# Layer norm's ScalarE part moved behind the last quad's normaliser, and shared products moved behind a mask product, in a two-layer-pair attention kernel

## The chip, the cores and the metric

The kernel runs on one core of a Trainium2 chip. The metric is device time in microseconds (us) of one execution; runs are repeated and their median is compared. The engines are TensorE (PE, with its weight loads shown apart as PEld), VectorE (DVE), ScalarE (ACT), GpSimd (POOL) and SyncE (SP), which issues transfers.

## What is computed

The reference applies four blocks to 2048 tokens of width 640: A, B, A, B, each as x = x + block(layernorm(x)), both A with the same weights and both B too.

```python
x = x + _A_ref(_layernorm(x), A_mem0, A_Wq, A_Wk, A_Wv, A_Wo, seg)
x = x + _B_ref(_layernorm(x), B_wqkv, B_wo)
x = x + _A_ref(_layernorm(x), A_mem0, A_Wq, A_Wk, A_Wv, A_Wo, seg)
x = x + _B_ref(_layernorm(x), B_wqkv, B_wo)
```

Block A works on 64 segments of 32 tokens, one after the other. Eight memory rows stand ahead of each segment, so it has 40 rows; 32 heads of width 192 attend over these rows under a mask, and the first eight output rows become the memory of the next segment. That recurrence is what makes the segments sequential. Block B has 32 heads of width 20 and looks back over 8 positions at a distance of 2. The layer norm has no weights: (x - m) / sqrt(v + eps).

## The kernel before

**Lanes and steps.** Both layer pairs run at once, as two lanes of 40 columns: lane 0 is the first pair, lane 1 the second, three segments behind (LAG). A step `t` does block A of segment `t` in lane 0 and of segment `t - 3` in lane 1, and parts of block B of the two steps before. There are 67 steps with block A, 61 of them (t = 3 to 63) with both lanes, the others with one, and two more that only finish block B.

**Quads.** A step goes over 8 quads of 4 heads (i = 0 to 7). Of each quad it makes K, Q and V (`a_k`, `a_q`, `a_v`; tiles ps_k, ps_q, ps_v), the scores (`a_s`: ps_s), their exponential E on ACT (L269), and E times the mask, Em, on DVE (L272). Then come, one quad later, P times V (`a_pv`: ps_o), the normaliser R on ACT, and the normalised output OT on DVE (`a_norm`); and one quad later still the output projection (`a_o`), which adds all quads into one PSUM bank, ps_acc.

**Normaliser.** V's tile has columns of ones, so ps_o holds the softmax sums beside the outputs. ACT takes four logarithms of them into R (L289) and one Exp with a factor of -1 (L291), which gives the reciprocals. DVE multiplies: one main product over all 128 partitions (L299), and two shared products (L300, L301) for the chunk whose halves belong to two heads, on partitions 0 to 63 and 64 to 127. ps_o has one buffer of two PSUM banks; R, E and Em have one buffer each, OT has two.

**Layer norm.** `ln1` prepares the next step's input: sums of x and of its squares by matmuls with ones (ps_st, L338), then on DVE the mean and the variance (L345 to L348), on ACT a logarithm and an Exp (ln_v, ln_r, L349 and L351), which give 1/sqrt(v + eps), on DVE x minus the mean (ln_xc, L356), and in `ln1_apply` the product with ln_r into the next step's input hT (L362, two instructions).

**End of a step.** After quad 6 the function `step` goes on, written out by hand: K and Q of quad 7, P times V of quad 6, V of quad 7, normalisation of quad 6, scores of quad 7, projection of quad 5, `ln1`, P times V and normalisation of quad 7, projection of quad 6, `ln1_apply`, block B's V and K (ps_bv, ps_bk, copied by ACT to VTB and KB), projection of quad 7, the new memory into hT (L326), x + A (L374), block B's Q (ps_bq) and a transpose of its V (ps_bvt). The next step begins with K of quad 0.

**Order.** The loop stands under a manual schedule for all five engines: each engine runs its instructions in the order in which the Python code issues them, and waits by semaphores for the others.

**Weights.** Block A's weights are 64 half units of 480 KB. 32 of them stay in SBUF; the other 32 are loaded again in each step by SP (L191) into a ring of six buffers (w_ring). All PSUM tiles of projections, statistics and block B share four banks in turn.

Of the kernel before, what the change touches and what calls it, by code (L numbers as in the profile page):

```python
# [61 lines left out]
class Kernel:  # L62
# [228 lines left out]
        nc.scalar.activation(out=rf, in_=rf, func=ACT.Exp, scale=-1.0)  # L291
        self.ov, self.r = ov, r

    def a_norm(self, i):
        nc = self.nc
        ov, r = self.cols(self.ov), self.cols(self.r[:])
        ot = self.ap2.tile([P, 2, 3, NT], BF16, name="OT")
        oc = self.cols(ot[:])
        nc.vector.tensor_tensor(out=oc[:, :, 0:3:2], in0=ov[:, :, 0:4:3], in1=r, op=ALU.mult)  # L299
        nc.vector.tensor_tensor(out=oc[0:64, :, 1], in0=ov[0:64, :, 1], in1=r[0:64, :, 0], op=ALU.mult)  # L300
        nc.vector.tensor_tensor(out=oc[64:P, :, 1], in0=ov[64:P, :, 2], in1=r[64:P, :, 1], op=ALU.mult)  # L301
        self.ots[i] = ot

    def a_o(self, i):
        nc = self.nc
# [35 lines left out]
    def ln_small(self, ps):  # L341

        nc = self.nc
        m = self.ap2.tile([P, NX], F32, name="ln_m")
        nc.vector.tensor_scalar(out=m[:], in0=ps[:, 0:NX], scalar1=1.0 / D, scalar2=None, op0=ALU.mult)  # L345
        v = self.bp.tile([P, NX], F32, name="ln_v")
        nc.vector.tensor_tensor(out=v[:], in0=m[:], in1=m[:], op=ALU.mult)
        nc.vector.scalar_tensor_tensor(out=v[:], in0=ps[:, NX:2 * NX], scalar=1.0 / D, in1=v[:], op0=ALU.mult, op1=ALU.subtract)  # L348
        nc.scalar.activation(out=v[:], in_=v[:], func=ACT.Ln, bias=self.eps_t[:])  # L349
        r = self.ap2.tile([P, NX], F32, name="ln_r")  # L350
        nc.scalar.activation(out=r[:], in_=v[:], func=ACT.Exp, scale=-0.5)  # L351
        return m, r
# [23 lines left out]
        self.bsq = self.ln_sq(x1)  # L376

    def b_ln(self, b):
        self.bmr = self.ln_small(self.ln_stats(self.x1[b], self.bsq))

    def b_ln_apply(self, b):
        dst = self.h2T[:, :, 64 * (b % 2):64 * (b % 2) + NX].rearrange("p c (l n) -> p c l n", l=2)
# [129 lines left out]

    def ln1(self, t):
        x = self.xin[t % 2]
        self.amr = self.ln_small(self.ln_stats(x, self.asq))
        self.axc = self.ln_center(x, self.amr)

    def ln1_apply(self, t):
        self.ln_scale(self.axc, self.amr, self.lanes(self.hT[t % 2][:, 0:NC * NT])[:, :, :, NM:LT])
# [1 line left out]
    def prologue(self):  # L521
        nc = self.nc
        self.xt, self.x1, self.ots, self.qxs = {}, {}, {}, {}
        self.x_load(0)
        nc.sync.dma_start(out=self.m0T[:], in_=self.mem0)
        nc.vector.tensor_copy(out=self.lanes(self.hT[0][:, 0:NC * NT])[:, :, 0, 0:NM], in_=self.m0T[:])
        self.x_take(0)
        self.ln1_sq(0)
        self.ln1(0)
        self.ln1_apply(0)  # L530
        self.build_mask_a()

    def step(self, t):
        T = self.n_seg + LAG
        self.set_lanes(t)
        b1 = t - 1 if 0 <= t - 1 < T else None
        b2 = t - 2 if 0 <= t - 2 < T else None
        nt = t + 1
        a = t < T
        for i in range(NQUAD - 1):  # L540
            if a:
                self.a_k(i, t)
                self.a_q(i, t)
                self.a_v(i, t)
                if i == 6:
                    self.a_pv(5)
                if i >= 2:
                    self.a_o(i - 2)
                if 1 <= i < 6:
                    self.a_pv(i - 1)  # L550
            if i == 0 and b1 is not None:
                self.b_ln(b1)
            if b2 is not None and i == 4:
                self.b_pv()
            if a and i >= 1:
                self.a_norm(i - 1)
            if b2 is not None and i == 6:
                self.b_wo(b2)
            if b2 is not None:
                if i == 0:  # L560
                    self.b_qexp(0)
                if 1 <= i <= 3:
                    self.b_s(b2, 2 * i - 2)
                    self.b_s(b2, 2 * i - 1)
                    if i < 3:
                        self.b_qexp(i)
                if i == 5:
                    self.b_ot()
            if i == 3 and b1 is not None:
                self.b_ln_apply(b1)  # L570
            if a:
                self.a_s()
            if t == 1 and i in (0, 3):
                self.load_b_weights(i)
            if t == 1 and i == 4:
                self.build_masks_b()
            if i == 1:
                if nt % 4 == 0 and nt < self.n_seg:
                    self.x_load(nt // 4)
                yseg = t - 3 - LAG  # L580
                if yseg >= 0 and yseg % 4 == 3:
                    self.y_store(yseg // 4)
            if i == 5 and nt < self.n_seg:
                self.x_take(nt)
        if a:
            self.a_k(7, t)
            self.a_q(7, t)
        if nt < T:
            self.ln1_sq(nt)
        if a:  # L590
            self.a_pv(6)
            self.a_v(7, t)
            self.a_norm(6)
            self.a_s()
            self.a_o(5)
        if nt < T:
            self.ln1(nt)
        if a:
            self.a_pv(7)
            self.a_norm(7)  # L600
            self.a_o(6)
        if nt < T:
            self.ln1_apply(nt)
        if b1 is not None:
            self.b_v(b1)
            self.b_k(b1)
        if a:
            self.a_o(7)
            if nt < T:
                self.mem_out(t)  # L610
            self.b_x1(t)
        if b1 is not None:
            self.b_q(b1)
            self.b_vt()
# [73 lines left out]
```

## Time and profile before

| what | value |
|---|---|
| runs: median (lowest to highest) | 3399.81 us (3399.69 to 3404.87), 3 runs |
| profiled execution: time, span | 3403.72 us, 3402.0 us |
| busy share of the span | PE 97%, PEld 85%, DVE 59%, ACT 61%, POOL 2% |
| mean granted clock of TensorE | 0.990 |
| transfers | 1088.74 MB, 320 GB/s in the mean; the weight queue 89.7% of the 16 engines' time |
| a step with both lanes, from K of quad 0 to K of quad 0 | 49.89 us |

A timeline line reads: start in us, time in us, engine, line of the kernel, operation, written tile <- read tiles, shapes, and count of merged instructions; in square brackets the idle time of the engine ahead of it and what ended that. A waits line reads: who waited for whom, total us, times, the longest. Matmuls overlap and their ends are modelled: a matmul of 80 columns is shown with about 0.20 us and the next one starts 0.036 us after it, so idle time of PE is best taken from start to start.

### The profile page before, as it was taken

Reading aid. Unit: us, or ns where it says so; the run is one execution under the profiler, and the core shown is the slowest. Engines: PE = TensorE matmul, PEld = TensorE weight load, DVE = VectorE, ACT = ScalarE, POOL = GpSimd, SP = SyncE. Lnnn points to the kernel's source line nnn. Section 1 sums busy time; section 2 is a strip of 40 time slices with the busy share of each in tenths; the row PEclk is TensorE's granted clock in tenths of the full one; section 3 lists DMA queues with packets and bytes.
Section 4 is the critical chain, followed back from the end, with each engine's and each line's share of the span. In section 5 each row is a group of like instructions: output and inputs, shape, how many; then the busy total and the mean of one; then the engine's idle time right before and its main releaser. Section 6 shows DMA issues by size and latency. Waiting matters only on the chain.

```text
span 3402.0 us, 164520 instructions
## 1 busy us (share of the span) xinstructions
PE 3284.0 (97%) x72896; PEld 2881.7 (85%) x72896; DVE 2004.8 (59%) x5841; ACT 2059.0 (61%) x6366; POOL 62.9 (2%) x188
## 2 busy tenths in 40 slices
PE   6899999999999999999999999999999999999997
PEld 4788888888888888888888888888888888888876
DVE  2456665665665666566566566656656656665654
ACT  2556666666666666666666666666666666666654
POOL 2000000000000000000000000000000000000000
PEclk7999999999999999999999999999999999999998
DMA  9989999999999999999999999999999999999995
GB/s 391 371 311 318 328 315 317 328 319 315 319 324 316 318 328 317 315 328 317 314 321 323 318 318 325 311 317 328 315 319 318 321 315 317 330 315 316 325 352 189
DMA packets 316123, 1088.74 MB, mean 320 GB/s; under 512 B 35504, under 2 KB 35632, under 8 KB 315280
## 3 DMA queue, kind: packets, MB, share of 16 engines
q1 hardware_dynamic: 313632, 1069.86, 89.7%
q8 instruction: 569, 9.32, 1.1%
q0 software_dynamic: 1776, 8.36, 0.8%
q14 instruction: 146, 1.20, 0.1%
HBM read 1075.46 MB, written 2.62 MB: 317 GB/s over the span
## 4 chain that ended last, share of the span: by engine, by line
PE 88%; ACT 5%; DMA 2%; issue 2%; DVE 2%; SPq 0%; POOLq 0%; ACTq 0%; POOL 0%
PE ps_v L251 25%; PE ps_k L221 16%; PE ps_q L221 16%; PE ps_acc L312 15%; PE ps_o L285 4%; ACT R L289 2%; PE ps_s L266 2%; PE ps_s L267 2%; DMA w_ring<-in_A_Wv_dram 2%; PE ps_bq L392 2%; PE ps_bs L441 2%; PE ps_by L486 1%; PE ps_st L338 1%; DVE OT L299 1%; ACT R L291 1%
## 5 line engine op out<-in xcount | busy, mean ns | idle before, releaser
L299 DVE TENSOR_TENSOR OT<-ps_o,R 128x320 bf16<-128x320 f32 (+1 forms) x536 | 255.3, 476 | 960.9 <-ACT R L291 949.4
L289 ACT ACTIVATE R<-ps_o 64x160 f32<-64x160 f32 (+1 forms) x2144 | 625.5, 292 | 307.3 <-PE ps_o L285 247.2
L251 PEld LDWEIGHTS <-hT 128*128 128x128 bf16 x5360 | 494.6, 99 | 298.3 <-issue 16.5
L221 PEld LDWEIGHTS <-w_ring 128*128 128x128 bf16 x16080 | 633.5, 100 | 13.8 <-issue 7.5
L257 ACT CAST Vt<-ps_v 80x384 bf16<-80x384 f32 x536 | 253.0, 472 | 566.5 <-PE ps_v L251 566.5
L251 PE MATMUL ps_v<-w_ring,hT 128*128 128x384 bf16 x2680 | 530.0, 329 | 9.3 <-DMA w_ring<-in_A_Wv_dram 7.7
L251 PE MATMUL ps_v<-w_v,hT 128*128 128x384 bf16 x2680 | 528.8, 329 | 3.1 <-DMA w_v<-in_A_Wv_dram 3.1
L312 PE MATMUL ps_acc<-OT,w_ring 128*128 128x80 bf16 (+1 forms) x8040 | 459.5, 200 | 43.8 <-DVE OT L299 37.8
L312 PE MATMUL ps_acc<-OT,w_o 128*128 128x80 bf16 (+1 forms) x8040 | 457.7, 200 | 4.5 <-issue 3.2
L239 DVE CAST QT<-ps_q 128x480 bf16<-128x480 f32 (+1 forms) x536 | 340.3, 635 | 184.9 <-PE ps_q L221 174.6
L312 PEld LDWEIGHTS <-w_ring 128*128 128x128 bf16 x8040 | 371.4, 99 | 85.6 <-issue 50.1
L221 PE MATMUL ps_q<-hT,w_ring 128*128 128x80 bf16 (+1 forms) x8040 | 370.5, 200 | 7.6 <-DMA w_ring<-in_A_Wq_dram 4.1
L221 PE MATMUL ps_k<-hT,w_k 128*128 128x80 bf16 (+1 forms) x8040 | 370.7, 200 | 6.4 <-DMA w_k<-in_A_Wk_dram 4.0
L221 PE MATMUL ps_q<-hT,w_q 128*128 128x80 bf16 (+1 forms) x8040 | 370.1, 200 | 5.9 <-DMA w_q<-in_A_Wq_dram 5.1
L221 PE MATMUL ps_k<-hT,w_ring 128*128 128x80 bf16 (+1 forms) x8040 | 369.9, 200 | 4.1 <-DVE hT L362 2.1
L312 PEld LDWEIGHTS <-w_o 128*128 128x128 bf16 x8040 | 350.6, 100 | 6.3 <-issue 4.6
L255 DVE CAST Vt<-ps_v 80x384 bf16<-80x384 f32 x536 | 293.6, 548 | 58.7 <-PE ps_v L251 58.7
L221 PEld LDWEIGHTS <-w_k 128*128 128x128 bf16 x8040 | 316.3, 100 | 7.5 <-DMA w_k<-in_A_Wk_dram 4.6
L221 PEld LDWEIGHTS <-w_q 128*128 128x128 bf16 x8040 | 316.0, 100 | 6.8 <-DMA w_q<-in_A_Wq_dram 5.9
L232 ACT CAST KF<-ps_k 128x320 bf16<-128x320 f32 (+1 forms) x536 | 217.9, 407 | 110.8 <-PE ps_k L221 110.8
L291 ACT ACTIVATE R<-R 128x320 f32<-128x320 f32 (+1 forms) x536 | 245.4, 458 | 17.0
L285 PE MATMUL ps_o<-Em,Vt 80*128 80x80 bf16 (+1 forms) x4288 | 239.5, 199 | 2.2 <-DVE Em L272 0.3
(99 smaller groups left out, 4100.0 us busy)
## 6 DMA issues: line engine op xcount, KB each, us to landing
w_ring<-in_A_Wk_dram SPq DMA_DIRECT2D x536, 480.0 KB, 5.4
w_ring<-in_A_Wq_dram SPq DMA_DIRECT2D x536, 480.0 KB, 5.4
w_ring<-in_A_Wv_dram SPq DMA_DIRECT2D x536, 480.0 KB, 5.3
w_ring<-in_A_Wo_dram SPq DMA_DIRECT2D x536, 480.0 KB, 5.6
w_k<-in_A_Wk_dram SPq DMA_DIRECT2D x8, 480.0 KB, 9.6
w_q<-in_A_Wq_dram SPq DMA_DIRECT2D x8, 480.0 KB, 9.6
w_v<-in_A_Wv_dram SPq DMA_DIRECT2D x8, 480.0 KB, 9.8
w_o<-in_A_Wo_dram SPq DMA_DIRECT2D x8, 480.0 KB, 9.7
```

The costliest lines, as they stand in the source:

```text
L221: nc.tensor.matmul(ps[:, NT * n + self.c0:NT * n + self.c1], lhsT=w[:, c, P * (n % 3):P * (n % 3 + 1)], rhs=hT[:, NT * c + self.c0:NT * c ...
L232: nc.scalar.copy(out=kf, in_=pv[:, :, 0:3:2, :])
L239: self.nc.vector.tensor_copy(out=self.cols(qt[:]), in_=self.cols(ps[:, 0:6 * NT].rearrange("p (a n) -> p a n", a=6)))
L251: nc.tensor.matmul(ps[:, 0:384], lhsT=hT[:, NT * c:NT * c + P], rhs=w[:, c, :], start=(c == 0), stop=(c == NC - 1))
L255: nc.vector.tensor_copy(out=dst, in_=src)
L257: nc.scalar.copy(out=dst, in_=src)
L266: nc.tensor.matmul(self.cols(sv[:, h]), lhsT=kf[:, NT * h:NT * h + P], rhs=self.cols(qt[:, 3 * pr + 2 * j]), start=True, stop=False)
L285: nc.tensor.matmul(self.cols(ov[:, pr, k]), lhsT=vt[0:NT, 512 * pr + c0:512 * pr + c0 + P], rhs=self.cols(em[0:NT, 2 * pr + k // 2]), star ...
L289: nc.scalar.activation(out=self.cols(r[r0:r0 + 64, :, j]), in_=self.cols(src), func=ACT.Ln)
L291: nc.scalar.activation(out=rf, in_=rf, func=ACT.Exp, scale=-1.0)
L299: nc.vector.tensor_tensor(out=oc[:, :, 0:3:2], in0=ov[:, :, 0:4:3], in1=r, op=ALU.mult)
L312: nc.tensor.matmul(self.acc[:, NT * c + self.c0:NT * c + self.c1], lhsT=w[m // 3][:, m % 3, P * c:P * (c + 1)], rhs=self.cols(ot[:, m]), s ...
```

## The change

Three things are reordered. `ln_small` is split: the DVE part stays in `ln1`, and the ACT part (ln_v, ln_r) is a function of its own, `ln_rstd`, which `step` calls after P times V and the normaliser of quad 7. At the start of the program and in block B's layer norm the two parts still follow each other. `a_norm` is split: for quad 6 alone the main product comes first, then the scores of quad 7 with E and Em, then the two shared products. By the build, the order of instructions on PE, POOL and SP is the same as before; only ACT's and DVE's at the end of a step differ. No instruction is added or removed, and no transfer.

```diff
-    def a_norm(self, i):
+    def a_norm(self, i, split=False):
...
+        self.norm = ov, r, oc
         nc.vector.tensor_tensor(out=oc[:, :, 0:3:2], in0=ov[:, :, 0:4:3], in1=r, op=ALU.mult)
+        self.ots[i] = ot
+        if not split:
+            self.a_norm_mid()
+
+    def a_norm_mid(self):
+
+        nc = self.nc
+        ov, r, oc = self.norm
         nc.vector.tensor_tensor(out=oc[0:64, :, 1], in0=ov[0:64, :, 1], in1=r[0:64, :, 0], op=ALU.mult)
         nc.vector.tensor_tensor(out=oc[64:P, :, 1], in0=ov[64:P, :, 2], in1=r[64:P, :, 1], op=ALU.mult)
-        self.ots[i] = ot
...
         nc.vector.scalar_tensor_tensor(out=v[:], in0=ps[:, NX:2 * NX], scalar=1.0 / D, in1=v[:], op0=ALU.mult, op1=ALU.subtract)
+        return m, v
+
+    def ln_rstd(self, m, v):
+        nc = self.nc
         nc.scalar.activation(out=v[:], in_=v[:], func=ACT.Ln, bias=self.eps_t[:])
...
     def b_ln(self, b):
-        self.bmr = self.ln_small(self.ln_stats(self.x1[b], self.bsq))
+        self.bmr = self.ln_rstd(*self.ln_small(self.ln_stats(self.x1[b], self.bsq)))
...
     def ln1(self, t):
         x = self.xin[t % 2]
-        self.amr = self.ln_small(self.ln_stats(x, self.asq))
-        self.axc = self.ln_center(x, self.amr)
+        self.amv = self.ln_small(self.ln_stats(x, self.asq))
+        self.axc = self.ln_center(x, self.amv)
+
+    def ln1_rstd(self):
+        self.amr = self.ln_rstd(*self.amv)
...
         self.ln1(0)
+        self.ln1_rstd()
         self.ln1_apply(0)
...
         if a:
             self.a_pv(6)
             self.a_v(7, t)
-            self.a_norm(6)
+            self.a_norm(6, True)
             self.a_s()
+            self.a_norm_mid()
             self.a_o(5)
         if nt < T:
             self.ln1(nt)
         if a:
             self.a_pv(7)
+        if nt < T:
+            self.ln1_rstd()
+        if a:
             self.a_norm(7)
             self.a_o(6)
```

## The prediction

> **What bounds the kernel now.** I read the busy shares first, then the waits of TensorE (PE), then the end of one step in the timelines of PE, ScalarE (ACT) and VectorE (DVE). The engine bound is PE; this row is 50 us from the middle:
>
> ```profile
> core 0: us, PE busy (x) PEld busy (x) DVE busy (x) ACT busy (x) POOL busy (x), PEclk, DMA share, GB/s
> ...
> 1000.00:1050.00 50.00, 49.37 (x1096) 43.64 (x1093) 30.25 (x87) 31.33 (x96) 0.41 (x1) 1.00 0.92 318
> ```
>
> PE is idle for 0.63 of 50 us, at full clock. The waits between 300 and 3300 us name one cause:
>
> ```profile
> PE ps_acc L312 <- DVE OT L299: 34.4, 58, 0.6
> PE ps_acc L312 <- issue: 5.3, 9, 1.1
> ...
> PE ps_o L285 <- DVE Em L272: 0.3, 1, 0.3
> ```
>
> So once in a step of 49.89 us the output projection waits 0.6 us for a normalised tile, and no weight transfer is waited for. The PE timeline of one step's end has it at quad 7:
>
> ```profile
> 1028.22 0.31 PE L338 MATMUL ps_st<-xin,ones 128*128 128x64 bf16 x5
> 1028.37 0.31 PE L338 MATMUL ps_st<-sq,ones 128*128 128x64 bf16 x5
> 1028.70 0.46 PE L285 MATMUL ps_o<-Em,Vt 80*128 80x80 bf16 x8
> ...
> 1030.81 1.04 PE L392 MATMUL ps_bk<-h2T,wqkv_sb 128*128 128x64 bf16 x30
> 1032.44 0.52 PE L312 MATMUL ps_acc<-OT,w_ring 128*128 128x80 bf16 x10 [0.60 <-DVE OT L299]
> ...
> 1033.51 1.04 PE L392 MATMUL ps_bq<-h2T,wqkv_sb 128*128 128x64 bf16 x30
> 1034.39 0.44 PE L420 MATMUL ps_bvt<-ident,VTB 128*128 128x128 bf16 x5
> ```
>
> The ends of matmuls are modelled, so I count from start to start. Thirty matmuls of this shape take 0.88 us (ps_bq to ps_bvt), so ps_bk leaves PE free at 1030.81 + 0.88 = 1031.69; the projection starts at 1032.44, a wait of **0.75 us**. A second one hides before ps_o: ten ps_st matmuls at 0.029 us leave PE free at 1028.51, and ps_o starts at 1028.70, 0.19 us later. No other change of group in the step has such a hole. Why quad 7 is late, ACT and DVE tell:
>
> ```profile
> 1027.47 0.43 ACT L269 ACTIVATE E<-ps_s 80x320 bf16<-80x320 f32 x1
> 1029.49 0.35 ACT L349 ACTIVATE ln_v<-ln_v,eps_t 128x64 f32<-128x64 f32 x1 [1.58 <-DVE ln_v L348]
> 1029.87 0.26 ACT L351 ACTIVATE ln_r<-ln_v 128x64 f32<-128x64 f32 x1
> 1030.14 1.23 ACT L289 ACTIVATE R<-ps_o 64x160 f32<-64x160 f32 x4
> 1031.40 0.47 ACT L291 ACTIVATE R<-R 128x320 f32<-128x320 f32 x1
> ```
>
> ```profile
> 1027.24 0.49 DVE L299 TENSOR_TENSOR OT<-ps_o,R 128x320 bf16<-128x320 f32 x1 [0.44 <-ACT R L291]
> 1027.65 0.30 DVE L300 TENSOR_TENSOR OT<-ps_o,R 64x160 bf16<-64x160 f32 x1
> 1027.97 0.33 DVE L301 TENSOR_TENSOR OT<-ps_o,R 64x160 bf16<-64x160 f32 x1
> 1028.33 0.32 DVE L272 TENSOR_TENSOR Em<-E,maskA 80x320 bf16<-80x320 bf16 x1
> ...
> 1031.90 0.49 DVE L299 TENSOR_TENSOR OT<-ps_o,R 128x320 bf16<-128x320 f32 x1 [2.04 <-ACT R L291]
> ```
>
> ACT sits idle 1.58 us for layer norm's variance, does ln_v and ln_r, and only then takes the logarithms of quad 7 (R, L289), though their ps_o was started at 1028.70.
>
> **Part 1: ln_v and ln_r behind R of quad 7.** Nothing is added or removed; the instruction orders of PE, POOL and SP stay, so no DMA is moved. Where ACT is free, R starts 0.54 us after ps_o (quad 6: 1024.94 to 1025.48). Here it starts 1.44 us after; 0.90 us goes from the chain. New chain, counted from ps_o: 0.54, four logarithms 1.26 (1030.14 to 1031.40), Exp to the main product 0.50 (to 1031.90), main product to the projection 0.54 (to 1032.44): **2.84 us**. PE itself is ready 1031.69 - 1028.70 = **2.99 us** after ps_o. So the chain falls 0.15 us behind PE's own work, and all of the 0.75 goes. What is late next is PE.
>
> What waits behind the moved pair: ln_r is wanted by DVE's hT products (L362), which stand behind the three products of quad 7 anyway: 1.80 + 0.50 + 0.41 + 0.32 + 0.36 = 3.39 us after ps_o, while ln_r is done by 1.80 + 0.50 + 0.38 + 0.26 = 2.94. Cover 0.45 us. Then VTB and KB on ACT: VTB now starts 3.07 us after ps_o and will start by about 3.0; the transposes that read it come 0.88 us after the projection's 1.07, near 4.9. Cover over 1 us. The next step's first matmuls need hT's memory columns (L326), which follow the projection and move with it; they end at 1033.95 against 1034.67. All three cost nothing; were the first cover gone, hT would start later by what is missing, with 0.7 us more before PE felt it.
>
> **Part 2: shared products of quad 6 behind Em of quad 7.** Em can start earlier, but ps_o lies in a single buffer, and the shared products (L300, L301) read quad 6's values from it. So ps_o of quad 7 has to wait for them as well, not for Em alone: a new wait, and PE is behind it. E ends at 1027.90, and Em starts 0.03 us after E where it waits for that alone (one-lane step: E ends at 3318.95, Em starts at 3318.98): 1027.93 to 1028.25, while the main product frees DVE at 1027.65. DVE idles 0.28 us there. Then the first shared product. It has no such predecessor in the trace, so there are two ends: it starts 0.08 us before Em's end, as it starts before the main product's (1027.65 against 1027.73, in all 488 two-lane cases), or 0.03 after, as the QT cast (L239) does behind Em in 304 cases. I take the first, since that row is the same instruction with the same operands, and the casts follow a shared product's read of rows 64 to 127. Then 1028.17; the second at +0.32, 1028.49; its end at +0.33, 1028.82; ps_o 0.06 later, as behind Em now: **1028.88 against 1028.70, 0.18 us later**. By the other end it is 1028.99, 0.29 later. It cannot fall below zero: Em and both products must end before ps_o, and the group gains an idle stretch.
>
> The Trainium skill, VectorE: DVE Perf Modes, section "Two Vector instructions with no wait between them", states a model by which an instruction waits for the one ahead to finish only when the start quadrant of an input or output differs from the last one used in that memory. The trace agrees where it can be seen (L301 starts 0.01 us after the end of L300, L300 starts 0.08 before the end of L299). By it the first shared product isn't held behind Em and the QT cast is, so it gives the 0.18; the nearest row after Em itself would give 0.29, 6.7 us more over the run.
>
> In the one-lane steps (t = 0 to 2 and 64 to 66), Em isn't what ps_o waits for: at t = 65 ps_o starts at 3319.32 with PE just free, and by the same count it would start near 3319.68; there the later projection waits only 0.05. Steps 1, 64 and 65 lose 0.3 to 0.4 each; steps 0 and 2, whose projections wait 1.7 and 0.8, gain 0.7 and 0.4; sum near 0, within 1 us.
>
> **The sum.** A two-lane step: 0.75 - 0.18 = 0.57, or 0.58 from unrounded times; there are 61 (t = 3 to 63): 35.4 us. Profiled execution: 3403.72 - 35.4 = 3368.3. That execution is 3.9 us above the median of the runs, and its step lengths show up to 1 us extra in some ten steps with no wait to name, so I set the forecast from the median: 3399.81 - 35.4 = **3364.4**. With the other end (0.29) it is 61 x 0.47 = 28.7, 3371.1.
>
> **Rivals.**
> *The stream of weights takes the gain.* Each step streams 32 x 480 KB = 15.7 MB, 315 GB/s over 49.89 us and 319 over 49.31. Against it: the first two 50 us windows moved 381 and 406 GB/s, PE waits for no transfer after 300 us, and each ring load there lands before its first matmul, 2 to 3 us in the median, 0.28 at the least. For it: the DMA share is 0.92, and a shorter tail gives less time to catch up. If it took all: 3400.
> The Trainium skill, Perfetto Trace Analysis, section "Engine Utilization", puts the HBM peak at 358 GB/s a core. The trace's 406 is above that, and measurement decides; by the page's figure too, an estimated 319 would fit, so the sum stays.
>
> *The chain still ends last.* The cover of 0.15 us is small. If R of quad 7 starts 0.3 to 0.5 us later than after quad 6, 0.15 to 0.35 us of the wait stay: 9 to 21 us less gain, 3374 to 3386.
>
> *Slower: the wait at ps_o.* The place is the single ps_o buffer between L301 of quad 6 and L285 of quad 7. It decides the sign once ps_o starts 0.75 us later than now, at 1029.45, that is when the shared products end 0.57 us later than I count. For it: in one-lane steps it already turns the sign, and Em hangs on E, which stands behind the Vt cast on ACT. Against: E isn't moved, and every duration is from its own row. If ps_o came 1.0 us late: 61 x 0.25 = 15 more, 3415.
>
> **How the numbers follow.** My forecast, with either start of the first shared product: 0.68 (3361 to 3372). Chain still last, or part of the gain lost to the stream: 0.14 (3372 to 3392). Gain gone: 0.06 (about 3400). Slower: 0.07 (about 3415). More than I count, below 3358: 0.05. About 0.2% (7 us) is what a measurement can tell from no change. So faster 0.68 + 0.14 + 0.05 = 0.87, same 0.06, slower 0.07. The range 3358 to 3380 takes in both ends of the unknown start, some 5 us of unnamed delays and the lower part of the second case.
>
> **What would show it.** Right: a two-lane step of 49.3 us; R of quad 7 0.54 us after ps_o with no ln_v before it; no wait of ps_acc for OT; a wait of ps_o for the second shared product (L310 in the changed file) of some 0.37 us from start to start, which the waits list shows as about 0.2, since modelled ends cover the rest; Em 0.03 us behind E. Wrong: ps_acc still waiting, DMA among PE's waits, or ps_o starting more than 0.3 us later against the statistics' matmuls than it does now.

## The result, and the profile after

| what | before | after |
|---|---|---|
| median of 5 runs (lowest to highest) | 3403.93 us (3399.69 to 3408.22) | 3387.1 us (3380.1 to 3396.55) |
| profiled execution: time, span | 3403.72, 3402.0 us | 3380.1, 3378.4 us |
| a two-lane step that nothing disturbs | 49.89 us | 49.32 us |
| mean of the 61 two-lane steps | 49.98 us | 49.57 us |

The ratio after to before is 0.9956 [0.9934, 0.9977]: 16.8 us less, where the prediction had 35.4. In the two profiled executions the difference is 23.6 us; that execution of after is the fastest of its five. The median of before was 3399.81 us over the three runs that the prediction started from and is 3403.93 over five, so 4.1 of the 22.7 us between the forecast of 3364.4 and the 3387.1 lie there.

Each view named in the prediction looks as it said. First the same 50 us from the middle, then the waits of PE from 300 to 3300 us (who waited <- for whom: total us, times, longest):

```profile
1000.00:1050.00 50.00, 49.78 (x1105) 44.06 (x1103) 31.04 (x90) 31.57 (x96) 0.41 (x1) 1.00 0.94 324
```

```profile
PE ps_o L285 <- DVE OT L310: 12.8, 59, 0.2
PE ps_acc L320 <- issue: 4.1, 4, 2.4
PE ps_q L221 <- issue: 3.5, 6, 1.3
PE ps_bk L404 <- issue: 3.3, 4, 1.1
PE ps_k L221 <- issue: 2.0, 2, 1.3
```

The 34.4 us of ps_acc for OT are gone, the new wait of ps_o is the 0.2 us once a step that was forecast, and no weight transfer is in the list. What is new lies in "issue", time in which PE waits for nothing that the profile shows. In the same stretch before, it was 9.3 us in 15 stops, 5.3 of them in one row (ps_acc). After, it is 16.6 us in 23, spread over nine rows of work that have nothing in common.

The end of a step, PE, ACT and DVE:

```profile
1020.09 0.46 PE L285 MATMUL ps_o<-Em,Vt 80*128 80x80 bf16 x8 [0.22 <-DVE OT L310]
...
1022.20 1.04 PE L404 MATMUL ps_bk<-h2T,wqkv_sb 128*128 128x64 bf16 x30
1023.07 0.52 PE L320 MATMUL ps_acc<-OT,w_ring 128*128 128x80 bf16 x10
```

```profile
1020.64 1.23 ACT L289 ACTIVATE R<-ps_o 64x160 f32<-64x160 f32 x4 [1.53 <-PE ps_o L285]
1021.90 0.47 ACT L291 ACTIVATE R<-R 128x320 f32<-128x320 f32 x1
1022.28 0.33 ACT L361 ACTIVATE ln_v<-ln_v,eps_t 128x64 f32<-128x64 f32 x1
```

```profile
1019.14 0.32 DVE L272 TENSOR_TENSOR Em<-E,maskA 80x320 bf16<-80x320 bf16 x1 [0.21 <-ACT E L269]
1019.39 0.31 DVE L309 TENSOR_TENSOR OT<-ps_o,R 64x160 bf16<-64x160 f32 x1
1019.71 0.33 DVE L310 TENSOR_TENSOR OT<-ps_o,R 64x160 bf16<-64x160 f32 x1
```

R of quad 7 starts 0.55 us after ps_o (forecast 0.54) with no ln_v ahead of it. The projection starts 0.87 us after ps_bk, so PE does not wait (over all two-lane steps, the start-to-start time from the last matmul of ps_bk to the first of ps_acc is 785 ns before, 29 ns after, in the median). From ps_st to ps_o the same count went from 224 to 411 ns: 0.19 us later, forecast 0.18. The first shared product starts 0.07 us before Em's end by the rounded rows, 0.08 in each of the 67 steps by unrounded times.

So the step came out as forecast to 0.02 us, and still half the gain is missing in the median and a third in the profiled execution. It is in the steps that are longer than 49.32: summed over the 61, what lies above the shortest step was 6.2 us before and is 15.5 us after. For the two profiled executions: 61 x 0.566 = 34.5 us gained, 9.3 of it lost in longer steps, and the first and last parts of the program together 1.6 us longer, which leaves the 23.6 measured.

**What a longer step looks like.** Here is one: PE in the timeline, then the same time in the chain that ended last (start, us, what):

```profile
1962.77 0.75 PE L404 MATMUL ps_bk<-h2T,wqkv_sb 128*128 128x64 bf16 x20
1964.62 0.45 PE L404 MATMUL ps_bk<-h2T,wqkv_sb 128*128 128x64 bf16 x10 [1.10 <-issue]
```

```profile
1962.93 0.58 PE ps_bk L404 x20
1963.52 1.10 issue
1964.62 0.45 PE ps_bk L404 x10
```

PE stops after 20 of 30 equal matmuls, with the operands of all thirty in SBUF for long, and goes on 1.26 us late. No data can be the reason. The page's table of DMA queues has, beside the weights' queue q1, two for instructions; the larger is q8 (q14 has 148 packets):

```profile
q1 hardware_dynamic: 313632, 1069.86, 90.6%
q8 instruction: 570, 9.34, 1.1%
```

The packets of q8 are of 16 KB. PE has 72,896 matmuls and as many weight loads; with 146 semaphore and drain instructions that is 145,938 records, and 145,938 / 570 = 256 to a packet. Counted from the start of the program, the 1964.62 matmul is record 84,417 = 329 x 256 + 193. All 24 stalls of over 0.2 us between 300 and 3250 us in after stand at record 193 or 194 of a 256 (the offset is that of the program's start), and so do 7 of 8 in before. They do not stand at one place of the step: a two-lane step has 2178 records, 8.5 blocks and 2 records, and the stalls move with that, from matmul 1043 of step 8 (in ps_acc) to matmul 993 of step 58 (in ps_bk), one matmul a step. A packet of q8 landed 1.40 us ahead of the 1964.62 matmul; it had started 3.35 us after PE began the block of 256 before.

That gives the reading (the *fetch theory*, F in the expectations; its plainest rival, N, is that the longer steps are chance): PE's instructions arrive in blocks of 256. In this kernel a block's transfer starts in the median 2.0 us after PE has begun the preceding block (up to 4.1), takes 0.96 us, and PE has never gone on less than 1.20 us after the landing. The sum is 4.2 us in the median case; when PE gets through the block ahead in less than the sum comes to, it waits. The 24 stalls agree: in each PE goes on 1.20 to 1.60 us after the landing, where a landing is 2.79 us ahead in the median of all blocks. A block lasts 5.88 us in the median; the blocks ahead of the 24 stalls, the stall itself taken off, lasted 4.5 us in the median (4.0 to 6.0), and their transfers started late, 3.0 us after the block before was begun. Blocks with the short matmuls of a step's end are the short ones: the one that comes in every second step around ps_bk and the last projection took 4.88 us before, of which 0.75 was the wait that the change takes out, and takes 4.16 after; its transfer landed 2.4 us ahead before, 1.6 after. In the steps between, the block there had its landing only 1.7 us ahead before, and 1.45 after.

### The profile page after: what moved, and what is told of

The parts are those of the page before. It is cut to its first block, busy times and chain, and to the rows that moved or that the text cites. A ratio compares the mean times of both kernels' runs of the same rounds, so it can differ in the third digit from the quotient of the medians.

```text
span 3378.4 us, 164785 instructions
## 1 busy us (share of the span) xinstructions
PE 3279.5 (97%) x72896; PEld 2878.9 (85%) x72896; DVE 2006.2 (59%) x5841; ACT 2061.5 (61%) x6366; POOL 63.1 (2%) x188
## 4 chain that ended last, share of the span: by engine, by line
PE 86%; ACT 5%; DMA 4%; issue 3%; DVE 2%; SPq 0%; POOLq 0%; ACTq 0%; POOL 0%
PE ps_v L251 22%; PE ps_k L221 16%; PE ps_q L221 15%; PE ps_acc L320 14%; PE ps_o L285 4%; DMA w_ring<-in_A_Wv_dram 3%; ACT R L289 2%; PE ps_s L266 2%; PE ps_s L267 2%; PE ps_bq L404 2%; PE ps_bk L404 2%; PE ps_bs L453 2%; PE ps_by L498 1%; PE ps_bv L424 1%; ACT Vt L257 1%
```

## The experiments

Ratios are to the kernel before, run on the same chip. "Clean step" is the shortest two-lane step of the profiled run, "stalls" is what PE loses between 300 and 3250 us in delays of over 0.1 us beyond a group's usual spacing (before: 5.6 us in 13; after: 18.8 in 37). Each total is that of one profiled execution; two executions of one kernel, after and again, have 18.8 and 30.8, so smaller differences than that are not read.

### The change again, and its two parts alone

`again` is the changed kernel unedited. `ln_only` is part 1 without part 2, `mid_only` part 2 without part 1:

```diff
 # ln_only
-            self.a_norm(6, True)
+            self.a_norm(6)
             self.a_s()
-            self.a_norm_mid()
 # mid_only: ln_rstd ahead of P times V of quad 7 again
+            self.ln1_rstd()
             self.a_pv(7)
-            self.ln1_rstd()
```

> The changed kernel once more, unedited, on the chip of the next three. Its profile had two-lane steps of 49.32 us where nothing unnamed happens (before: 49.89), as summed, but some 18.8 us of PE stalls that no semaphore explains between 300 and 3250 us (before: 5.3 us). Theory F (instruction supply): these stalls belong to the change, since PE's instructions come in blocks of 16 KB and the removed wait had given the block at the step's end its time; the ratio stays at 0.995 +- 0.002, clean steps are 49.32, stalls 12 to 30 us. Rival N (chance): the stalls are noise of that one chip and hour; here they fall to 3 to 8 us and the ratio to 0.989 to 0.991.

> Part 1 alone: ln_v and ln_r behind quad 7's normaliser, the three products of quad 6 together as before. My sum: no new wait at ps_o, so a clean two-lane step is 49.89 - 0.75 = 49.14 us and, with no stalls, the time 46 us below before (ratio 0.9865). F: the step's end is 0.17 us shorter still, so the stalls grow again, 20 to 40 us in the profile, and the ratio is 0.992 to 0.997, little or nothing better than the full change. N: ratio 0.986 to 0.989.

> Part 2 alone: shared products of quad 6 behind Em, layer norm's ACT part at its old place ahead of quad 7's logarithms. My sum: ps_o 0.18 us later and the chain through ln_m, ln_v, ln_r and R later by 0.15, so the wait of ps_acc stays and a clean two-lane step is 50.04 us; time 9 us above before, ratio 1.002 to 1.004. F: the wait at the step's end is there again, so stalls are as few as before, 3 to 9 us. N says nothing else of this run.

| | median, us | ratio | clean step | stalls |
|---|---|---|---|---|
| again | 3391.9 | 0.9963 [0.995, 0.9975] | 49.31 | 30.8 us in 56 |
| ln_only | 3378.24 | 0.9921 [0.9907, 0.9934] | 49.13 | 27.5 in 44 |
| mid_only | 3421.49 | 1.0046 [1.0033, 1.0059] | 50.03 | 15.8 in 24 |

The stalls belong to the kernel and not to one execution: again has 45 of its 46 over 0.2 us at the same place of a block, ln_only 36 of 39, mid_only 22 of 22. The clean steps are those of the sum to 0.02 us. Part 1 alone is worth 49.89 - 49.13 = 0.76 a step, 46 us, and 27 arrive. Part 2 alone costs 0.14 a step: the wait of ps_acc stays (753 ns instead of 785) and ps_o starts 0.18 later. Its waits of PE:

```profile
PE ps_acc L320 <- DVE OT L300: 27.0, 50, 0.6
PE ps_o L285 <- DVE OT L310: 12.8, 59, 0.5
```

So **part 1 alone is the better kernel**: 13.7 us under the full change on the same chip. For the fetch theory mid_only is a miss: the wait stays, and 3 to 9 us of stalls were expected, not 15.8. Its 22 stalls of over 0.2 us stand behind longer blocks than those of after (5.1 us in the median without the stall, against 4.5), and the transfers started later (3.5 us, against 3.0); why they were late more often than in the kernel before is open. With 5.6 and 15.8 us where the wait stays and 18.8 to 30.8 where it goes, these runs alone do not show that the stalls come from taking out the wait.

### No stream of weights

Ring loads after the first six are left out, and PE reads the tiles that lie there, in the kernel before and in the changed one. So most streamed weights are never loaded, while the instructions of all engines but SP stay:

```diff
+            self.n_ring = getattr(self, "n_ring", 0) + 1
+            if self.n_ring > RING:
+                return self.kept[self.n_ring % RING]...
```

> The kernel before without the stream of weights: the first six ring loads are made, and every later use of a ring buffer reads what lies there, so most streamed weights are wrong and the output is not the reference's. All engines' instructions but SP's loads stay. The run's beginning, where PE waits for transfers, gets shorter in both kernels of this pair, some 20 to 40 us. F with contention: PE's instruction blocks no longer stand behind weight packets; a block's transfer starts about 1 us after the block before it is begun instead of 1.9, and unnamed stalls in the middle fall from 5 to 9 us to under 2. F without contention: start and stalls stay as they are.

> The changed kernel without the stream of weights, with the same omission. F with contention: stalls fall from 16 to 31 us to under 4, clean steps stay 49.32, and it is 33 to 37 us faster than the kernel before without the stream, which is the gain that I forecast. F without contention (a block needs its 4 us whatever else moves): stalls stay at 15 to 30 us, and the difference is 10 to 20 us as between the two kernels with the stream.

Before: 3347.54 us, ratio 0.9837 [0.9822, 0.9852]; after: 3308.75, 0.9726 [0.9712, 0.9739]. That is 38.8 us between them, the 35 of the sum and some 4 from the one-lane steps and the ends (147.3 to 145.4 us up to step 3, 155.7 to 154.0 from step 64). The steps lie 0.5 and 0.2 us in all above the shortest; the stalls are 0.8 and 0.9 us. The waits of PE, first of before without the stream, then of after without it:

```profile
PE ps_acc L317 <- DVE OT L304: 35.7, 60, 0.6
PE ps_o L290 <- DVE Em L277: 0.3, 1, 0.3
```

```profile
PE ps_o L290 <- DVE OT L315: 13.6, 61, 0.5
PE ps_bs L458 <- DVE QX L448: 6.6, 5, 1.4
```

No "issue" is left (the QX row belongs to the program's end). The instruction packets are as many and as long, 569 of 1.0 us; the queues of after without the stream:

```profile
q1 hardware_dynamic: 5760, 18.85, 1.5%
q8 instruction: 569, 9.32, 1.2%
```

But now a block's transfer starts 0.2 to 0.3 us after the block before has begun, in the median, instead of 1.9 to 2.0 (some 1 us was expected). So the whole gain of the sum is there when no weights stream, and the loss comes with the stream, though in after PE waits for no weight between 300 and 3300 us. This run alone does not tell instruction blocks from any other effect of the stream; the next pair does.

### Fewer instructions with the stream kept

Block B's projections are done by half as many matmuls of twice the width (V by 15 instead of 25): 40 matmuls and 40 weight loads fewer in a step. The other column groups are left out, so block B's values are not the reference's; the kernel serves for its times alone.

```diff
-        for n in range(NBC):
+        for n in range(NBC // 2):
...
-                nc.tensor.matmul(ps[:, NX * n:NX * (n + 1)], ..., rhs=h[:, c, :],
+                nc.tensor.matmul(ps[:, P * n:P * (n + 1)], ..., rhs=self.h2T[:, c, :],
```

> The changed kernel with block B's projections as half as many matmuls over twice the columns: 15 matmuls instead of 25 for ps_bv, 15 instead of 30 for ps_bk and for ps_bq, most over all 128 columns of h2T; the other column groups are left out, so block B's values are not the reference's. PE time stays (15 x 57 ns for 30 x 29 ns), but 80 of PE's 2176 instructions of a step are gone, all at the step's end. F: blocks at the step's end last 0.5 to 0.9 us longer, stalls fall to 0 to 6 us, ratio 0.988 to 0.991. N: fewer instructions change nothing; stalls and ratio are those of the unedited change in this call.

> The kernel before with block B's projections as half as many matmuls over twice the columns, with the same omission of column groups as in wide_after; 80 of PE's instructions of a step are gone and PE's time at the step's end falls by about 0.1 us. A control: the old wait stays, since the chain through ACT sets it, so a clean step stays within 0.1 us of 49.89. F: there is little to win, as the wait already gave the fetch its time: stalls under 6 us, ratio 0.996 to 1.000, so that the change is worth 35 us or more between wide_before and wide_after. If instead fewer instructions make any version faster by much, the ratio here is under 0.992, as wide_after's is lower by other means than stalls.

After: 3353.57 us, 0.9849 [0.9835, 0.9862], stalls 10.0 us in 18, steps 5.8 us above the shortest in all; that is faster than the 0.988 to 0.991 expected, with more stalls than the 0 to 6 us expected. Before: 3395.56, 0.9978 [0.9969, 0.9988], stalls 4.5, steps 2.9 above. The queue q8 now has 549 packets instead of 570. The change is worth 42 us between these two (44 by the ratios), with all weights streaming. The matmuls' work at a step's end is the same to 0.1 us (clean steps 49.21 and 49.85); that 0.1, which the old wait hides in before, gives some 4 of the 42. Fewer instructions carry the work, so a block lasts longer there (6.0 us in the median of all, and none under 4.4, where 23 of after are under 4.2). A stream that held back PE's data would have held it back here too.

### Blocks moved against the step

`shift` puts 32 matmuls, 64 records, at the program's start, so that each block begins elsewhere in the step:

```diff
+        ps = self.big("ps_pad")
+        for _ in range(32):
+            nc.tensor.matmul(ps[:, 0:P], lhsT=self.ident[:], rhs=self.ident[:], start=True, stop=True)
```

> The changed kernel with 32 matmuls (64 PE instructions) into a spare bank at the program's start. Nothing else differs; they cost under 5 us, while the first weights are still on their way. F: PE's instruction blocks now begin 64 instructions earlier in the step. Stalls stay 16 to 35 us, but they stand at other matmuls: counted by PE's instructions from the program's start they keep their place in the block of 256, counted from the step's start they move by 64, so the stalls that stood in quad 0's K and Q (after the step's end) and in the projection of quad 4 or 5 stand 32 matmuls earlier. If a place in the step is at fault (a semaphore, a bank, a load), they stay at their matmuls.

3383.5 us, 0.9942 [0.9929, 0.9956], stalls 24.8 us in 52, the clean step unchanged at 49.32. 36 of 37 stalls over 0.2 us are again at 193 or 194 of 256 *counted from the program's start*, and within the step they have moved ahead by the 32 matmuls: the stall in K or Q of quad 0 stood at matmul 59 of step 33 and 35 of step 57, and now stands at 27 and 3. A stall is thus tied to the instruction's place in the stream of instructions, and not to what it computes. That closes the case for blocks. The time itself moves little (0.9942 against 0.9956 and 0.9963); that some short block lies near the step's end either way is my reading of it, not tested.

### A longer block ahead

`v_late` moves V of quad 7, which has the longest matmuls, to where the gap of the step's end is, and two thirds of the projection of quad 5 in its place; both copies of that V go to ACT:

```diff
             self.a_pv(6)
-            self.a_v(7, t)
+            self.a_o(5, 0)
             self.a_norm(6, True)
             self.a_s()
             self.a_norm_mid()
-            self.a_o(5)
+            self.a_v(7, t)
+            self.a_o(5, 1)
```

> The changed kernel with V of quad 7 moved behind the scores of quad 7, and two thirds of the projection of quad 5 ahead of them; both copies of that V on ACT. No instruction is added or removed and the output is the reference's. V has long matmuls (10 in 1.63 us), so the run of short ones at the step's end, about 530 PE instructions in some 9 us, is cut into about 350 and 460. Em is then early, and ps_o of quad 7 waits 0.1 us or less: a clean step of 48.95 to 49.05 us. F: blocks at the step's end last longer, stalls of 5 to 15 us, ratio 0.983 to 0.988. If the order of long and short matmuls plays no part: stalls of 20 us or more as in the change, ratio 0.988 to 0.992.

3400.45 us, 0.9998 [0.9986, 1.001]: a miss (0.983 to 0.988 was expected, with 5 to 15 us of stalls). The clean step is the shortest of all versions that compute the whole (49.09), yet the stalls are 47.4 us in 63, 51 of 54 at block bounds. One of them:

```profile
2620.63 0.49 PE L406 MATMUL ps_bq<-h2T,wqkv_sb 128*128 128x64 bf16 x11
2622.49 0.71 PE L406 MATMUL ps_bq<-h2T,wqkv_sb 128*128 128x64 bf16 x19 [1.38 <-issue]
```

What I had not counted: the block ahead loses the long matmuls that the later one gains (5.69 to 4.84 us), and the transfer for the step's end starts later, 2.4 instead of 1.6 us after the block before has begun. The first is plain; why the start is later is not settled.

### A smaller stream

Part 1 alone, with 33 or 34 half units resident and a ring of 5 or 4 (38 tiles in SBUF, as before), so that 31 or 30 are streamed:

```diff
-N_RES = 32
-RING = 6
+N_RES = 33      # ring4_part1: 34
+RING = 5        # ring4_part1: 4
```

> Part 1 alone (as ln_only) with 33 resident half units and a ring of 5 in place of 32 and 6, in the same SBUF. The stream falls by 3%, and one load fewer can stand ahead of an instruction block. F: stalls fall from 27 us to 12 to 24, clean steps stay 49.13 us; ratio 0.988 to 0.992 unless weights come late: the ring's lead falls from some 9 to 7.8 us against 5.4 to landing, so PE waits for w_ring appear, up to 10 us. If the queue ahead has no part in the stalls, they stay at 25 us or more and the ratio at 0.992 or above.

> The same with 34 resident half units and a ring of 4: the stream falls by 6%, at most about three loads stand in the queues. F: instruction stalls fall to 2 to 12 us. But the ring's lead is some 6.6 us, 1 us above the time to landing, so weights are waited for in the middle of the steps, 10 to 60 us in the profile; the ratio is between 0.987 and 1.005, whichever is larger. If the queue ahead has no part in it, instruction stalls stay above 20 us.

Ring 5: 3395.86 us, 0.9976 [0.9963, 0.9989]. Ring 4: 3502.25, 1.0286 [1.0267, 1.0304]. With ring 5 the stalls at block bounds do not fall (27.4 us in 41, against 26.6 in 41 in ln_only; transfers of blocks start at 1.84 us against 1.87), a miss: 3% less stream does not let instructions through sooner. Its profiled execution is 12.8 us longer than that of ln_only: PE waits 5.3 us for weights between 300 and 3300 us, and the part up to step 3 takes 6.5 us more. With ring 4 the start falls to 1.55 us and the stalls at block bounds to 18.9 us in 35, not to the 2 to 12 us expected; and now weights are waited for, 71 us in all, where 10 to 60 were expected:

```profile
PE ps_acc L320 <- DMA w_ring<-in_A_Wo_dram: 26.8, 36, 1.7
PE ps_v L251 <- DMA w_ring<-in_A_Wv_dram: 24.3, 34, 1.7
```

The two kinds of wait look different, then, and what after has is not this one.

### Short matmuls taken out of the step's end

Part 1 alone, with 20 of the 30 matmuls of ps_bq moved behind V of quad 0 of the next step:

```diff
+            if i == 0 and b2 is not None:
+                self.b_q(b2, 2, NBC)
...
-            self.b_q(b1)
+            self.b_q(b1, 0, 2)
```

> Part 1 alone with two thirds of block B's Q (20 of 30 short matmuls, 40 PE instructions) moved from the step's end behind V of quad 0 of the next step, where PE's block lasts 7.4 us because V's matmuls are long. One ACT copy more in a step; the output is the reference's. PE's work is the same; the next step's K needs the new memory 0.52 us after the last projection, and 0.57 of short matmuls are left there: a clean step of 49.13 to 49.20 us. F: of the two blocks a pair of steps that lie in the step's end, one takes in V and lasts 1 us longer: stalls fall from 27 to 12 to 22 us; ratio 0.988 to 0.991 against 0.992 of ln_only. If spreading is of no use, as v_late had it, stalls stay at 25 us or more and the ratio at 0.992 or above.

3374.16 us, 0.9912 [0.9899, 0.9926], stalls 20.4 us in 38 (ln_only 27.5 in 44), the clean step the same 49.13 and now the median too. The lowest ratio of the versions that compute the whole, but it was run on another chip than ln_only (0.9921 [0.9907, 0.9934]) and the intervals overlap, so that it is better is not shown; and 20.4 against 27.5 us of stalls is a difference that two executions of one kernel can have.

## Why the prediction was wrong

**Part 1** was right in every number: R 0.55 us after ps_o, the wait of 0.75 gone, and nothing late next on ACT or DVE (mid_only against again: 50.03 - 49.31 = 0.72 with part 2 in both; ln_only: 0.76).

**Part 2** was right in kind and size: ps_o 0.19 us later. The choice between the two starts of the first shared product fell to the right side: 0.08 us ahead of Em's end. The rule from the Trainium skill, VectorE: DVE Perf Modes, section "Two Vector instructions with no wait between them", agrees with this row, which is what it was asked for. What I did not draw from my own sum is that part 2 costs 11 us and gains nothing: ln_only shows it.

**The covers** of hT, of VTB and KB held: in after PE has no recurring wait for any of them. The sum of the one-lane steps, forecast near 0 within 1 us, did not: the first and last parts are 1.6 us longer in the profiled execution with the stream, and 3.6 shorter without it. There the projection waited 0.84 us in steps 1, 2, 64 and 65 before and 0.03 after, while the prediction had read 0.05 at t = 65 with the stream, in a step that took 46.7 us there and takes 41.1 without it. So without the stream the difference is 38.8 us, 3 to 4 more than forecast.

**The step that failed** is in the sum: "its step lengths show up to 1 us extra in some ten steps with no wait to name, so I set the forecast from the median", and "some 5 us of unnamed delays" in the range, as if these were a property of the run that the change would not touch. Most of them are waits of PE for its own instructions, and with the shorter step's end they grew: the steps lie 15.5 us above the shortest in all (24.9 in again), not 6.2. So the term that was held constant at some 5 us took 9.3 us of the gain in the profiled execution. With that goes "What is late next is PE": next after the chain came PE's instruction blocks. The 5.3 us row of "issue" in the waits of before was the sign (2.5 of it lie before 3250 us, the rest in the one-lane steps), and it stood in the first fence of the waits. One question to the trace, which record of the program each stop is, would have shown 7 of the 8 before 3250 us at 193 or 194 of 256. The same question would have shown the block at the step's end landing 2.4 us ahead with 1.25 the least seen, so that only about 1.2 us, less the spread of the transfers' start (0.8 to 3.0 us in 9 of 10), was left there, for a cut of 0.58.

**The rivals.** "The stream of weights takes the gain" was right that the stream decides, and its partial form (3372 to 3392) held the median of 3387.1. That is luck: its mechanism, a weight that comes late, did not occur. After has no such wait between 300 and 3300 us, the ring loads land 2.2 to 3.1 us ahead of their first matmul in the median as they did before (2.3 to 3.2), and the wide kernels get 42 us with the same stream. "The chain still ends last" did not come: PE goes from ps_bk to the projection in 29 ns. The wait at ps_o came as costed, and far from the price at which it would decide the sign.

**Open.** Why a block's transfer starts 1.9 us after the block before has begun when weights stream and 0.2 to 0.3 us when not, which part of the path holds it, and why in v_late and mid_only it starts later for some blocks. Why executions of after spread from 3380 to 3397: with the landing so near the least that PE needs, small shifts of a transfer count, but that is argued, not shown. A version that computes the whole and has no stalls was not found; a PE program with fewer instructions for the same result was not tried.

## What to carry to other kernels

When a wait is taken out of a stretch of short matmuls, count how many instructions PE has to get through there in how many microseconds, and compare with how fast the profile shows them arriving: here 256 in 4.2 us in the median case. Time that the profile puts down to "issue" was not noise here; look up which instruction of the program each stop is before holding it constant. And when two parts of a change have their own terms in the sum, and one of them is a pure loss, price the other alone.

## What the runs showed of the hardware

- PE's instructions, matmuls and weight loads alike, come in packets of 16 KB on the queue q8, 256 to a packet (64 bytes each), 0.96 us a packet. Beside a weight stream at a DMA share of 0.92 to 0.93 the next packet starts 1.9 to 2.0 us after PE has begun the block before, in the median, without the stream 0.2 to 0.3 us; beside it PE has gone on about 1.2 us after a landing at the earliest.
- PE stalls when it gets through a block in less time than the next one's start, transfer and those 1.2 us take together, 4.2 us in the median case of after; late transfers stalled it behind blocks of up to 6.0 us too. Between 300 and 3250 us the stalls are 5.6 us in the kernel before, 18.8 to 30.8 in the changed one, 47.4 in v_late, and 0.9 in the changed kernel without the stream (none of that at a block bound).
